# The steps of a chunked scan in another order around a split-precision MLP, and the halves of its output regrouped

## The chip, the cores and the metric

One core of a Trainium2 chip runs the whole program. The metric is the device time of one execution in microseconds. The profile is of one execution on the chip.

## The reference

A chunked state-space scan (Mamba2 SSD) is followed by an MLP with SiLU. Per batch and head, for each chunk of 32 positions:

```
cum = cumsum(log(clip(a)))             # x (4,8,768,32), a (4,8,768), B and C (4,8,768,16)
M   = (C B^T) * exp(cum_i - cum_j) * causal
y   = M x + (C state) * exp(cum)
state = exp(sum la) * state + sum_j B_j x_j * exp(cum_last - cum_j)
```

y is laid out as 3072 tokens of 256 values, and out = silu(y w_in) w_out, with w_in 256 x 2048 and w_out 2048 x 256, all fp32.

## The kernel before

**Units and pairs.** The scan works on twelve units of 256 positions, three to a batch, each in four chunks of 64. The MLP works on six pairs of two units, 512 tokens each. Every engine's instructions are in the order in which the program writes them (the schedule is manual), so an instruction that waits holds all that stand behind it on its engine. Each DMA queue is in order too; nearly all loads and all stores are on the sync engine's queue.

**The steps of a unit**, by the letters of the program's strings: L loads it. T transposes B and C (VectorE; for units 1 and 2 TensorE, in a PSUM tile tp) and ScalarE makes ce from ct. P makes the decay prefix pfx (VectorE). 0, 1, 2 make the decay matrix E: 0 clips a, 1 and 2 are two scans of VectorE. B makes BT from E's last column, C makes cw from ct (both GpSimd as a rule). G and g are the two halves of C B^T on TensorE, here called G(0) and G(1), into the one two-bank PSUM tile gy. M and m, here M(0) and M(1), multiply that half into E in place (VectorE). D makes the chunks' state sums on TensorE, S the running states and, before the change, also sm, two activations. Y and y are the two halves of the output on TensorE, each followed by X, a copy to xf (ScalarE). h, l, d split xf into three fp32r parts: xh (ScalarE), xl (GpSimd), xd (VectorE). E, BT, ce, cw and sm have one buffer each, and so has gy.

**The first pair's MLP** is in plain fp32 matmuls: f_s1 (16 calls, into hp) and f_s2 (m0 to m7, into oa). The scan of units 2 and 3 and the preparation of the weights are written between them by hand: w_size and w_bits bring the weights (s, b), and w_h, w_l, w_d split them into WH, WL, WD (h, l, d with a number, or wh, wl, wd in rows). f_out stores the result by way of o and ot; then the loads of units 4 and 5 are issued.

**The other five pairs**, 1 to 5, run in steps of one 128-column tile of d_ff: sixteen steps to a pair, f = 0 to 15. A step holds twelve 128x512 matmuls: four in s1_h, two in s1_d for the next step, whose result ScalarE scales in place before s1_h may add to it, and six in s2 of three steps earlier (LAG). Between them stand g and gh (ScalarE), gl (GpSimd) and gd (VectorE). At its end step f takes stage f of PLAN for the first unit of the next pair and stage f - 6 for its second unit:

```
    PLAN = ("T", "P0", "12GBC", "Mg", "mD", "S", "Y", "y", "hld")
...
            for i, base in enumerate((0, 6)):
                if 0 <= f - base < len(PLAN):
                    u = 2 * P + 2 + i
                    stage(u, PLAN[f - base])
```

So in step 8 the first unit's h, l, d are written ahead of the second unit's stage 2. f_out of a pair comes in step 2 of the next pair, after that step's s2; it holds two od on ScalarE and o, ot, o, ot on VectorE, and the next pair's s2 accumulates in the banks that od and o read.

Of the kernel before, what the change touches and what calls it, by code (L numbers as in the profile page):

```python
# [12 lines left out]
AF = mybir.ActivationFunctionType  # L13
# [18 lines left out]
def kernel(  # L32
# [22 lines left out]
    nc = tc.nc  # L55

    batch, H, S, D = x.shape
    N = B.shape[-1]
    Q = 64
    UT = 256  # L60
    UPB = S // UT
    NU = batch * UPB
    d_model, d_ff = moe_w_in.shape
    NF = d_ff // 128
# [88 lines left out]
    NW = 16  # L153
# [4 lines left out]
    def two(t):  # L158
        return t.rearrange("p (k f) -> p k f", k=2)
# [36 lines left out]
    def w_h(n):  # L196
        WH[n] = block("wh", F32R)
        nc.scalar.activation(WH[n], w32[n], AF.Copy, scale=DOWN / 4096.0)

    def w_l(n):  # L200
        WL[n] = block("wl", F32R)
        nc.vector.scalar_tensor_tensor(out=WL[n], in0=WH[n].bitcast(FP32), scalar=-4096.0, in1=w32.pop(n),
                                       op0=ALU.mult, op1=ALU.add)

    def w_d(n, engine=nc.gpsimd):
        WD[n] = block("wd", F32R)
        engine.tensor_tensor(out=WD[n], in0=WH[n].bitcast(FP32), in1=WL[n].bitcast(FP32), op=ALU.subtract)
# [207 lines left out]
    def f_S(u, t0=0, t1=4):  # L415
        first, last = u % UPB == 0, u % UPB == UPB - 1
        if first and t0 == 0:
            ST[u] = sc2.tile([128, 4, 64], FP32, name="st")
        if not last and t1 == 4:
            ST[u + 1] = sc2.tile([128, 4, 64], FP32, name="st")  # L420
        for t in range(t0, min(t1, 3 if last else 4)):
            k, c = divmod(t, 2)
            o = ST[u][:, t + 1] if t < 3 else ST[u + 1][:, 0]
            if first and t == 0:
                nc.vector.tensor_copy(out=o, in_=BX[u][c][:, k])
            else:
                nc.vector.scalar_tensor_tensor(out=o, in0=ST[u][:, t], scalar=PFX[u][:, t, Q:],
                                               in1=BX[u][c][:, k], op0=ALU.mult, op1=ALU.add)

    def f_SM(u):  # L430
        t0 = 1 if u % UPB == 0 else 0
        SM[u] = sc.tile([128, 4, 64], FP32, name="sm")
        for e in range(2):
            nc.scalar.activation(SM[u][:, t0:, 32 * e:32 * e + 32], ST[u][:, t0:, 32 * e:32 * e + 32],
                                 AF.Copy, scale=par[:, e:e + 1])

    def f_Y(u, w):
        sp, cw, m, xc = SM[u], CW[u], E[u], xt[u]
        y = GY[u] = bank2()
        opened = set()  # L440
        for t in ((1, 2, 3) if w == 0 else (2, 1, 3)) if u % UPB == 0 else range(4):
            k, c = divmod(t, 2)
            for q in range(2):
                g = 2 * w + q
                nc.tensor.matmul(out=y[64 * q:64 * q + 64, c, 64 * k:64 * k + 64],  # L445
                                 lhsT=sp[32 * g:32 * g + 32, t], rhs=cw[32 * g:32 * g + 32, Q * t:Q * t + Q],
                                 start=(c, q) not in opened, stop=False,
                                 tile_position=(32 * g, 64 * q), skip_group_check=True)
                opened.add((c, q))
        for k in range(2):  # L450
            for c in range(2):
                for q in range(4):
                    h = 4 * w + q
                    nc.tensor.matmul(out=y[32 * q:32 * q + 32, c, 64 * k:64 * k + 64],
                                     lhsT=xc[64 * c:64 * c + 64, k, h], rhs=m[64 * c:64 * c + 64, k, h],
                                     start=False, stop=True, tile_position=(64 * c, 32 * q), skip_group_check=True)

    def f_X(u, w):

        if w == 0:  # L460
            XF[u] = block("xf")
        y = GY.pop(u)
        nc.scalar.activation(two(XF[u])[:, w].rearrange("p (k c t) -> p c k t", k=2, c=2),
                             y[:, :, 0:128].rearrange("p c (k t) -> p c k t", k=2), AF.Copy)


    XH, XL, XD = {}, {}, {}
# [46 lines left out]
    G, GH, GL, GD, HP = {}, {}, {}, {}, {}  # L514

    def s1_d(s):
        P, f = 1 + s // NF, s % NF
        HP[s] = half("hp")
        for kc in range(KC):
            nc.tensor.matmul(out=HP[s], lhsT=two(WD[f // 2])[:, kc, 128 * (f % 2):128 * (f % 2) + 128], rhs=XD[P][:, kc],  # L520
                             start=(kc == 0), stop=False, skip_group_check=True)
        nc.scalar.activation(HP[s], HP[s], AF.Copy, scale=-1.0 / UP)  # L522

    def s1_h(s):
        P, f = 1 + s // NF, s % NF
        for kc in range(KC):
            for i, (w, x_) in enumerate(((WH, XH), (WL, XL))):
                nc.tensor.matmul(out=HP[s], lhsT=two(w[f // 2])[:, kc, 128 * (f % 2):128 * (f % 2) + 128],  # L528
                                 rhs=x_[P][:, kc], start=False, stop=(kc == KC - 1 and i == 1), skip_group_check=True)
        if f == NF - 1:  # L530
            for X in (XH, XL, XD):
                X.pop(P)
# [109 lines left out]
    def stage(u, what):  # L642
        for c in what:
            if c == "L":
                load_unit(u)
            elif c == "T":
                if 0 < u < UPB:
                    f_TP(u)
                else:
                    f_T(u, 0)  # L650
                    f_T(u, 1)
                f_T2(u, 0)
                f_T2(u, 1)
            elif c == "P":
                f_P(u)
            elif c == "0":
                f_E0(u, 0, 1)
            elif c in "12":
                f_E1(u, int(c) - 1, 2)
            elif c == "B":  # L660
                f_B(u)
            elif c == "C":
                f_C(u)
            elif c in "Gg":
                f_G(u, "Gg".index(c))
            elif c in "Mm":
                f_M(u, "Mm".index(c))
            elif c == "D":
                f_D0(u)
            elif c == "S":  # L670
                f_S(u)
                f_SM(u)
            elif c in "Yy":
                f_Y(u, "Yy".index(c))
                f_X(u, "Yy".index(c))
            elif c == "h":
                f_xh(u)
            elif c == "l":
                f_xl(u)
            elif c == "d":  # L680
                f_xd(u)

    def todo(text):

        for step in text.split():
            if ":" in step:
# [3 lines left out]
            n = int(step[1:].split(".")[0])  # L690
            {"b": w_bits, "s": w_size, "h": w_h, "l": w_l, "d": w_d, "m": f_s2, "o": partial(f_out, 0)}[step[0]](n)

    steps = ((1, 0, ""), (0, 3, "b5 s6"), (1, 1, "b6 s7"), (1, 2, "b7 s8"), (1, 3, "b8"), (0, 4, ""),
             (1, 4, "2:T"), (0, 5, "2:P012 2:B s9"), (1, 5, "2:CG b9 s10 2:M"), (0, 6, "2:g"), (1, 6, "b10 s11 2:m"),
             (0, 7, "2:D b11 2:S s12"), (1, 7, "2:Yy b12 s13"))
    for u, j, text in steps:
        f_s1(u, j)
        todo(text)
    stage(3, "L")
    for text in ("m0 2:h h0 2:l l0 2:d b13 s14", "m1 d0 b14 s15", "m2 h1 b15 3:T", "m3 l1 d1 3:P012", "m4 3:BC 3:G",  # L700
                 "m5 3:Mg 3:m h8 3:D l8 d8", "m6 3:S 3:Y", "m7 3:y 3:h 3:l 3:d h2 l2 d2 h9 l9 d9 o0 o1"):
        todo(text)
    stage(4, "L")
    stage(5, "L")
# [1 line left out]

    NP = NU // 2
    LAG = 3
    PLAN = ("T", "P0", "12GBC", "Mg", "mD", "S", "Y", "y", "hld")
    WAITING = []  # L710

    def step(s):

        last = NF * (NP - 1)
        if s < last:
            if s == 0:
                s1_d(0)
            s1_h(s)
            if s + 1 < last and (s + 1) % NF:
                s1_d(s + 1)  # L720
            s1_g(s)
            s1_gl(s)
        if s >= LAG:
            s2(s - LAG)
        if s - 1 >= 0 and s - 1 < last:
            s1_gd(s - 1)
        if s >= LAG and (s - LAG) % NF == NF - 1:
            P = 1 + (s - LAG) // NF
            f_out(P, 0)
            f_out(P, 1)  # L730
        if s >= last:
            return
        P, f = 1 + s // NF, s % NF
        if P + 1 < NP:
# [3 lines that stand above are left out]
                    stage(u, PLAN[f - base])  # L738
                    if PLAN[f - base] == "y" and u + 2 < NU:
                        load_unit(u + 2)  # L740
        if P == 1 and f % 2 == 0:
            for n in (3 + f // 2, 10 + f // 2):
                if n < (8 if n == 3 + f // 2 else NW):
                    w_h(n)
                    w_l(n)
                    w_d(n)
        if s + 1 < last and (s + 1) % NF == 0:
            s1_d(s + 1)

# [33 lines left out]
```

## Time and profile before

| | before |
|---|---|
| time, median of two runs | 461.23 us (460.69 to 461.77) |
| time of the profiled execution | 462.7 us |
| its span | 460.7 us |
| TensorE busy | 378.4 us (82%) |
| VectorE, ScalarE, GpSimd busy | 221.4 (48%), 213.1 (46%), 183.5 us (40%) |
| mean granted clock of TensorE | 0.904 of full speed |

The span lies inside the execution, which takes 2.0 us more. A matmul's row ends some time after the next one may start, so distances are read from start to start. PE is TensorE's matmuls, DVE VectorE, ACT ScalarE, POOL GpSimd and SP the sync engine's queue.

### The profile page before, as it was taken

To read this page: it belongs to the slowest core of one execution; us is meant where nothing else is said; L and a number is where in the kernel's file an instruction comes from. 1 tells how busy PE (TensorE), PEld (TensorE's weight loads), DVE (VectorE), ACT (ScalarE), POOL (GpSimd) and SP (SyncE) were. 2 spreads that over 40 slices of the span, in tenths; PEclk is the share of its full clock that TensorE was granted. 3 is DMA by queue.
4 is the path that set the end of the run, shared out by engine and by line. 5 is a ranking of instruction groups with operands and counts; after the bars stand their busy time and mean duration, and the time that the engine had idled before them with its cause. 6 is when DMAs were issued, how large, how long until landed. Compare 5 with 4: busy or idle time off the path is not lost. (4 is left out here: it accounts for less than half of the span.)

```text
span 460.7 us, 7904 instructions
## 1 busy us (share of the span) xinstructions
PE 378.4 (82%) x3145; PEld 284.1 (62%) x3146; DVE 221.4 (48%) x343; ACT 213.1 (46%) x403; POOL 183.5 (40%) x160
## 2 busy tenths in 40 slices
PE   7898989952499397969699769969787969799993
PEld 3577778731376275747477547657565747577882
DVE  7689659224858734354421463342364442324222
ACT  2567461043358074626336434616452625365660
POOL 3344344233667544323434242433333343334440
PEclk9999999977789798879979888979798989889998
DMA  8879630026650400044140035140011000002002
GB/s 183 185 198 278 171 55 1 1 35 127 125 104 27 82 9 0 2 87 74 35 81 1 0 65 96 36 81 3 0 19 28 1 1 1 1 0 47 0 1 46
DMA packets 112620, 26.35 MB, mean 57 GB/s; under 512 B 102216, under 2 KB 108360, under 8 KB 112584
## 3 DMA queue, kind: packets, MB, share of 16 engines
q1 hardware_dynamic: 110504, 25.73, 26.7%
q8 instruction: 24, 0.39, 0.4%
q10 hardware_dynamic: 2080, 0.13, 0.3%
q14 instruction: 12, 0.10, 0.1%
HBM read 22.70 MB, written 3.15 MB: 56 GB/s over the span
## 5 line engine op out<-in xcount | busy, mean ns | idle before, releaser
L542 POOL TENSOR_TENSOR gl<-g,gh 128x512 fp32r<-128x512 f32 x80 | 104.2, 1303 | 165.7 <-ACT gh L538 147.4
L546 DVE SCALAR_TENSOR_TENSOR gd<-gl,gh 128x512 fp32r<-128x512 f32 x80 | 61.5, 774 | 142.7 <-POOL gl L542 139.1
L522 ACT ACTIVATE hp<-hp 128x512 f32<-128x512 f32 x80 | 46.5, 582 | 160.2 <-PE hp L520 160.2
L528 PE MATMUL hp<-xh,wh 128*128 128x512 f32 x160 | 75.8, 474 | 12.2 <-ACT hp L522 12.2
L528 PE MATMUL hp<-xl,wl 128*128 128x512 f32 x160 | 70.1, 438 | 0.0
L520 PE MATMUL hp<-xd,wd 128*128 128x512 f32 x160 | 57.7, 446 | 13.5 <-DVE xd L483 13.5
L560 PE MATMUL oa<-gh,wh 128*128 128x512 f32 x160 | 65.8, 411 | 0.4 <-DVE o L570 0.4
L561 PE MATMUL oa<-gl,wl 128*128 128x512 f32 x160 | 65.0, 406 | 0.0
L557 PE MATMUL oa<-gd,wd 128*128 128x512 f32 x160 | 54.6, 424 | 0.1
L407 PE MATMUL gy<-ce,bh 32*64 32x128 f32 x384 | 19.6, 323 | 41.3 <-DVE E L413 41.3
L538 ACT ACTIVATE gh<-g 128x512 fp32r<-128x512 f32 x80 | 50.5, 631 | 3.7
L528 PEld LDWEIGHTS hp<-xh,wh 128*128 128x128 f32 x160 | 33.9, 212 | 28.0 <-ACT hp L522 16.5
L520 PEld LDWEIGHTS hp<-xd,wd 128*128 128x128 f32 x160 | 34.0, 215 | 23.6 <-DVE xd L483 15.4
L536 ACT ACTIVATE g<-hp 128x512 f32<-128x512 f32 x80 | 47.5, 593 | 1.0 <-PE hp L528 0.6
L407 PEld LDWEIGHTS gy<-ce,bh 32*64 32x64 f32 x384 | 12.7, 155 | 49.9 <-DVE E L413 42.8
L557 PEld LDWEIGHTS oa<-gd,wd 128*128 128x128 f32 x160 | 33.4, 209 | 9.0 <-DVE o L570 0.5
L560 PEld LDWEIGHTS oa<-gh,wh 128*128 128x128 f32 x160 | 32.3, 202 | 9.4 <-DVE o L570 1.8
L528 PEld LDWEIGHTS hp<-xl,wl 128*128 128x128 f32 x160 | 34.4, 215 | 5.9
L561 PEld LDWEIGHTS oa<-gl,wl 128*128 128x128 f32 x160 | 31.8, 199 | 7.6
L191 POOL TENSOR_TENSOR w<-wu,wv 128x512 uint32<-128x512 uint32 (+1 forms) x20 | 21.7, 1093 | 31.9 <-DVE wv L186 30.9
L493 PE MATMUL hp<-xf,w 128*128 128x256 f32 x128 | 30.1, 386 | 2.6 <-DVE cw L375 1.8
L483 DVE SCALAR_TENSOR_TENSOR xd<-xl,xh 128x512 fp32r<-128x512 f32 x10 | 11.1, 1106 | 41.7 <-POOL xl L479 41.7
(82 smaller groups left out, 452.9 us busy)
## 6 DMA issues: line engine op xcount, KB each, us to landing
ab<-in_a_dram SPq DMA_DIRECT2D x40, 128.0 KB
raw<-in_moe_w_in_dram SPq DMA_DIRECT2D x8, 512.0 KB
raw<-in_moe_w_out_dram SPq DMA_DIRECT2D x8, 512.0 KB
xt<-in_x_dram SPq DMA_DIRECT2D x24, 128.0 KB
out_dram<-ot SPq DMA_DIRECT2D x48, 64.0 KB
bn<-in_B_dram SPq DMA_DIRECT2D x22, 64.0 KB
tbc<-in_C_dram SPq DMA_DIRECT2D x40, 32.0 KB
pa<-in_a_dram SPq DMA_DIRECT2D x10, 128.0 KB
```

The lines of the kernel that those rows point to most:

```text
L407: nc.tensor.matmul(out=GY[u][64 * c:64 * c + 64, q, 128 * k:128 * k + 128], lhsT=bh[32 * g:32 * g + 32, ts], rhs=ce[32 * g:32 * g + 32, :, ...
L493: nc.tensor.matmul(out=hp[:, i], lhsT=two(w32[j])[:, kc, 128 * i:128 * i + 128], rhs=two(XF[u])[:, kc], start=(kc == 0), stop=(kc == KC - 1))
L520: nc.tensor.matmul(out=HP[s], lhsT=two(WD[f // 2])[:, kc, 128 * (f % 2):128 * (f % 2) + 128], rhs=XD[P][:, kc], start=(kc == 0), stop=Fals ...
L522: nc.scalar.activation(HP[s], HP[s], AF.Copy, scale=-1.0 / UP)
L528: nc.tensor.matmul(out=HP[s], lhsT=two(w[f // 2])[:, kc, 128 * (f % 2):128 * (f % 2) + 128], rhs=x_[P][:, kc], start=False, stop=(kc == KC ...
L536: nc.scalar.activation(G[s], HP.pop(s), AF.Silu, scale=UP)
L538: nc.scalar.activation(GH[s], G[s], AF.Copy, scale=DOWN)
L542: nc.gpsimd.tensor_tensor(out=GL[s], in0=G.pop(s), in1=GH[s].bitcast(FP32), op=ALU.subtract)
L546: nc.vector.scalar_tensor_tensor(out=GD[s], in0=GL[s].bitcast(FP32), scalar=-4096.0, in1=GH[s].bitcast(FP32), op0=ALU.mult, op1=ALU.add)
L557: nc.tensor.matmul(out=OA[P][1][m], lhsT=two(WD[n])[:, r, ms], rhs=gd, start=(f == 0), stop=(f == NF - 1))
L560: nc.tensor.matmul(out=OA[P][0][m], lhsT=two(WH[n])[:, r, ms], rhs=gh, start=(f == 0), stop=False)
L561: nc.tensor.matmul(out=OA[P][0][m], lhsT=two(WL[n])[:, r, ms], rhs=gl, start=False, stop=(f == NF - 1))
```

## The change

The program writes the scan's stages in another order, in the five pairs' PLAN and in the hand-written part before it. T and P go into one stage, E, its scans and B into the next, then G(0), C and M(0), then G(1) and M(1), then D and S; sm is a stage of its own (s). Unit 3's loads and steps are written earlier in the first pair's part. Weight parts 3 to 7 are made in the first pair's second product and not in pair 1; parts 10 to 15 are made in two steps each. In the step in which a pair's last s2 comes, that s2 is written ahead of s1_h. And f_Y(u, e) makes, where it made four heads over both chunk parities, both head halves w, each at chunk parity w ^ e, one PSUM bank to a head half; so the first sixteen matmuls take four row and column tiles of the array by turns instead of two. f_X copies a bank at a time, in two activations instead of one.

```diff
-    def f_Y(u, w):
+    def f_Y(u, e):
...
-        for t in ((1, 2, 3) if w == 0 else (2, 1, 3)) if u % UPB == 0 else range(4):
-            k, c = divmod(t, 2)
-            for q in range(2):
-                g = 2 * w + q
-                nc.tensor.matmul(out=y[64 * q:64 * q + 64, c, 64 * k:64 * k + 64],
-                                 lhsT=sp[32 * g:32 * g + 32, t], rhs=cw[32 * g:32 * g + 32, Q * t:Q * t + Q],
-                                 start=(c, q) not in opened, stop=False,
-                                 tile_position=(32 * g, 64 * q), skip_group_check=True)
-                opened.add((c, q))
         for k in range(2):
-            for c in range(2):
+            for w in range(2):
+                t = 2 * k + (w ^ e)
+                if t == 0 and u % UPB == 0:
+                    continue
+                for q in range(2):
+                    g = 2 * w + q
+                    nc.tensor.matmul(out=y[64 * q:64 * q + 64, w, 64 * k:64 * k + 64],
+                                     lhsT=sp[32 * g:32 * g + 32, t], rhs=cw[32 * g:32 * g + 32, Q * t:Q * t + Q],
+                                     start=(w, q) not in opened, stop=False,
+                                     tile_position=(32 * g, 64 * q), skip_group_check=True)
+                    opened.add((w, q))
+        for k in range(2):
+            for w in range(2):
+                c = w ^ e
                 for q in range(4):
                     h = 4 * w + q
-                    nc.tensor.matmul(out=y[32 * q:32 * q + 32, c, 64 * k:64 * k + 64],
+                    nc.tensor.matmul(out=y[32 * q:32 * q + 32, w, 64 * k:64 * k + 64],
                                      lhsT=xc[64 * c:64 * c + 64, k, h], rhs=m[64 * c:64 * c + 64, k, h],
                                      start=False, stop=True, tile_position=(64 * c, 32 * q), skip_group_check=True)
 
-    def f_X(u, w):
+    def f_X(u, e):
...
-        nc.scalar.activation(two(XF[u])[:, w].rearrange("p (k c t) -> p c k t", k=2, c=2),
-                             y[:, :, 0:128].rearrange("p c (k t) -> p c k t", k=2), AF.Copy)
+        o = two(XF[u]).rearrange("p w (k c t) -> p w k c t", k=2, c=2)
+        for w in range(2):
+            nc.scalar.activation(o[:, w, :, w ^ e], y[:, w, 0:128].rearrange("p (k t) -> p k t", k=2), AF.Copy)
...
             elif c == "S":
                 f_S(u)
+            elif c == "s":
                 f_SM(u)
...
-    steps = ((1, 0, ""), (0, 3, "b5 s6"), (1, 1, "b6 s7"), (1, 2, "b7 s8"), (1, 3, "b8"), (0, 4, ""),
-             (1, 4, "2:T"), (0, 5, "2:P012 2:B s9"), (1, 5, "2:CG b9 s10 2:M"), (0, 6, "2:g"), (1, 6, "b10 s11 2:m"),
-             (0, 7, "2:D b11 2:S s12"), (1, 7, "2:Yy b12 s13"))
+    steps = ((1, 0, ""), (0, 3, "b5 s6"), (1, 1, "b6 s7"), (1, 2, "b7 s8"), (1, 3, "b8"), (0, 4, "2:T"),
+             (1, 4, "2:P0"), (0, 5, "2:12B s9 3:L"), (1, 5, "2:GCM b9 s10"), (0, 6, "2:gm"), (1, 6, "2:DS b10 s11"),
+             (0, 7, "2:s 2:Y b11 s12"), (1, 7, "2:y b12 s13 3:T"))
...
-    stage(3, "L")
-    for text in ("m0 2:h h0 2:l l0 2:d b13 s14", "m1 d0 b14 s15", "m2 h1 b15 3:T", "m3 l1 d1 3:P012", "m4 3:BC 3:G",
-                 "m5 3:Mg 3:m h8 3:D l8 d8", "m6 3:S 3:Y", "m7 3:y 3:h 3:l 3:d h2 l2 d2 h9 l9 d9 o0 o1"):
+    for text in ("m0 2:h h0 3:P0 2:l b13 s14", "m1 3:12B 2:d h1 l0 d0 b14 s15", "m2 3:GCM l1 d1 h2", "m3 3:gm b15 l2 d2 h3",
+                 "m4 3:DS l3 d3 h4", "m5 3:s 3:Y l4 d4 h5", "m6 3:y 3:h 3:l l5 d5 h6 3:d h8", "m7 l8 l6 d8 d6 h7 h9 l7 l9 d7 d9 o0 o1"):
...
-    PLAN = ("T", "P0", "12GBC", "Mg", "mD", "S", "Y", "y", "hld")
+    PLAN = ("TP", "012B", "GCM", "gm", "DS", "s", "Y", "y", "hld")
...
+            if s >= LAG and (s - LAG) % NF == NF - 1:
+                s2(s - LAG)
             s1_h(s)
...
-        if s >= LAG:
+        if s >= LAG and (s >= last or (s - LAG) % NF != NF - 1):
             s2(s - LAG)
...
-        if P == 1 and f % 2 == 0:
-            for n in (3 + f // 2, 10 + f // 2):
-                if n < (8 if n == 3 + f // 2 else NW):
-                    w_h(n)
-                    w_l(n)
-                    w_d(n)
+        n = 10 + f // 2
+        if P == 1 and n < NW:
+            if f % 2 == 0:
+                w_h(n)
+            else:
+                w_l(n)
+                w_d(n)
```

## Rows read from the trace of the kernel before

**Rows 1.** Second product, pair 1, pair 3 by windows: busy us (instructions), clock:

```profile
61.38:97.48 36.10, 31.92 (x290) 26.62 (x281) 19.72 (x29) 10.80 (x22) 12.30 (x11) 0.98 0.01 1
99.37:183.25 83.88, 57.99 (x487) 42.08 (x487) 48.40 (x59) 38.52 (x73) 47.16 (x35) 0.85 0.38 70
256.96:328.89 71.93, 60.40 (x497) 45.03 (x497) 29.76 (x50) 33.85 (x64) 26.62 (x22) 0.88 0.24 45
```

**Rows 2.** List of waits: engine, line, tile, awaited; us in total, times, longest:

```profile
PE gy L407 <- DVE E L413: 41.3, 10, 7.9
...
PE hp L493 <- DVE cw L375: 1.8, 1, 1.8
```

**Rows 3.** TensorE, pair 3, steps 9 to 11: start us, us, instruction, [idle before]:

```profile
298.26 0.39 PE L561 MATMUL oa<-gl,wl 128*128 128x512 f32 x1
302.92 1.15 PE L407 MATMUL gy<-ce,bh 32*64 32x128 f32 x16 [4.27 <-DVE E L413]
...
309.09 0.50 PE L528 MATMUL hp<-xh,wh 128*128 128x512 f32 x1
...
311.98 0.39 PE L528 MATMUL hp<-xh,wh 128*128 128x512 f32 x1
```

**Rows 4.** Timeline of VectorE and GpSimd in the same stretch:

```profile
296.78 1.30 POOL L479 TENSOR_TENSOR xl<-xf,xh 128x512 fp32r<-128x512 f32 x1
...
298.12 0.69 DVE L483 SCALAR_TENSOR_TENSOR xd<-xl,xh 128x512 fp32r<-128x512 f32 x1 [4.54 <-POOL xl L479]
...
298.73 2.33 DVE L314 TENSOR_TENSOR_SCAN E<-ab,diag 128x512 f32<-128x512 f32 x2
...
301.14 1.00 POOL L347 TENSOR_TENSOR BT<-bn,E 128x256 f32<-128x256 f32 x1 [3.05 <-DVE E L314]
```

**Rows 5.** Timeline of VectorE and GpSimd at the end of pair 3:

```profile
325.60 1.28 POOL L542 TENSOR_TENSOR gl<-g,gh 128x512 fp32r<-128x512 f32 x1
325.69 1.73 DVE L483 SCALAR_TENSOR_TENSOR xd<-xl,xh 128x512 fp32r<-128x512 f32 x1 [4.38 <-POOL xl L479]
```

**Rows 6.** Timeline of pair 3, steps 2 to 4, three engines:

```profile
267.31 1.06 ACT L569 ACTIVATE od<-oa 128x512 f32<-128x512 f32 x2
...
267.48 0.50 PE L528 MATMUL hp<-xh,wh 128*128 128x512 f32 x1
...
267.92 0.69 DVE L570 SCALAR_TENSOR_TENSOR o<-oa,od 128x512 f32<-128x512 f32 x1 [0.76 <-ACT od L569]
...
268.65 0.71 DVE L572 STREAM_TRANSPOSE ot<-o 128x512 f32<-128x512 f32 x1
...
274.76 1.15 PE L407 MATMUL gy<-ce,bh 32*64 32x128 f32 x16 [4.04 <-DVE E L413]
```

**Rows 7.** Timeline from the first pair's end to step 2 of pair 1:

```profile
97.48 1.22 PE L520 MATMUL hp<-xd,wd 128*128 128x512 f32 x2 [3.30 <-DVE xd L483]
...
98.55 1.30 DVE L572 STREAM_TRANSPOSE ot<-o 128x512 f32<-128x512 f32 x2
...
99.28 4.40 SPq L574 DMA_DIRECT2D out_dram<-ot  x8
...
109.67 0.64 DVE L352 STREAM_TRANSPOSE ct<-tbc 128x256 f32<-128x256 f32 x1 [0.96 <-DMA tbc<-in_C_dram]
...
112.82 0.80 PE L528 MATMUL hp<-xh,wh 128*128 128x512 f32 x1 [8.18 <-ACT hp L522]
```

**Rows 8.** Timeline of TensorE, step 3 of pair 1:

```profile
125.65 1.15 PE L407 MATMUL gy<-ce,bh 32*64 32x128 f32 x16 [5.87 <-DVE E L413]
```

**Rows 9.** Timeline of TensorE in pair 3, one Y and what follows:

```profile
287.05 0.68 PE L445 MATMUL gy<-cw,sm 32*64 32x64 f32 x16
287.66 0.45 PE L454 MATMUL gy<-E,xt 64*32 64x64 f32 x32
288.04 0.50 PE L528 MATMUL hp<-xh,wh 128*128 128x512 f32 x1
```

**Rows 10.** Timeline of TensorE in the opening:

```profile
12.19 0.68 PE L407 MATMUL gy<-ce,bh 32*64 32x128 f32 x16 [2.07 <-DVE E L413]
```

More of the change, by code (lines that the diff above doesn't have):

```diff
@@ L452, in f_Y @@
+        for k in range(2):
+            for w in range(2):
+                c = w ^ e
                 for q in range(4):
                     h = 4 * w + q
-                    nc.tensor.matmul(out=y[32 * q:32 * q + 32, c, 64 * k:64 * k + 64],
+                    nc.tensor.matmul(out=y[32 * q:32 * q + 32, w, 64 * k:64 * k + 64],
                                      lhsT=xc[64 * c:64 * c + 64, k, h], rhs=m[64 * c:64 * c + 64, k, h],
                                      start=False, stop=True, tile_position=(64 * c, 32 * q), skip_group_check=True)
-    def f_X(u, w):
-        if w == 0:
+    def f_X(u, e):
+        if e == 0:
```

## The prediction, made before the change was run

> **What bounds the kernel now.** I read the busy table first: TensorE is busy 82% of the span, the others under half. So TensorE sets the time, and what counts is its idle time and its clock. The windows by stage come next. Pair 1 takes 83.9 us and pair 3 71.9 us, each with a mean granted clock of 0.85 to 0.88 [rows 1]. A step that carries no scan work takes 2.89 us at full clock (two starts of the xh matmul, 309.09 and 311.98) [rows 3], so sixteen take 46 us. The scan's own matmuls explain few of the other 26 us of pair 3. The list of waits names the rest: TensorE stands 41.3 us, in ten waits, ahead of G(1), because VectorE's M(0) is late [rows 2]. 2.6 us of that lie in the opening (one of 2.07 us stands in [rows 10]); the other 38.7 are 5.87 [rows 8] and 7.90 [rows 2] in pair 1 and 4.04 [rows 6] and 4.27 [rows 3] in each of pairs 2 to 4. A second cost follows each: from G(1) at 302.92 to the second step after it TensorE takes 6.17 us [rows 3], where G(1) at 0.68 [rows 10], one step of 2.89 and a D of 0.38 (32 small matmuls, as in [rows 9]) make 3.95. So a long wait costs 2.2 us more at the low one of TensorE's two clocks.
>
> Why M(0) is late, the timelines of VectorE and GpSimd show: xl ends 298.08, then xd, then two E scans of 2.33 us together, then BT of 1.00 on GpSimd, which must read E before M(0) overwrites it [rows 4]. All of that stands between TensorE's arrival (298.26 plus one matmul) and its G(1).
>
> **The change, part by part.**
>
> *The scan's steps in a pair.* E, its two scans and BT move one step earlier, and M(0) goes into the step of G(0), ahead of G(1) by a whole step. What is late then?
>
> Second unit of a pair (steps 8 and 9). In step 8 VectorE still has xd of the first unit ahead of M(0), since the first unit's last stage is written before the second's. E has one buffer, so the scans can't start before the first unit's second Y is done, at the start of step 8; they and BT (1.00) then push gl and xl by up to 0.9 us. M(0) follows xl (298.08) by xd, 0.69 alone [rows 4] or 1.73 beside a GpSimd operation [rows 5], and by its own 0.78 (BT's end to G(1), 302.14 to 302.92). That is 299.6 to 301.5; TensorE is there at 298.65. The wait of 4.27 becomes 0.9 to 2.9 us; I take 2.0, the middle, since both pushes are likely in part.
>
> First unit (steps 2 and 3). The scans are out of the way, but f_out isn't: od, o, ot, o, ot of the pair that ends stand ahead of M(0). And the last s2 now goes ahead of s1_h in step 2. ScalarE's queue has the next scale, g and gh of that step before od, and they wait for s1_h, which comes 1.4 us later (six matmuls, half a step). So od moves from 267.31 [rows 6] to 268.7; o follows by 0.6, the four VectorE operations take 2.7 (two of 0.69 and two of 0.71), M(0) ends at 272.8. TensorE has done step 3 at 270.3 (267.48 plus 2.8). Behind o wait the next pair's s2 matmuls, which need its accumulators, and behind M(0) G(1): together 2.5 us, for 4.04 now. Ends: 1.1 if f_out keeps its old time, 4.0 if nothing is gained.
>
> Pairs 2 to 4: 8.31 becomes 4.5, so -3.8 each, **-11.4**. Pair 1 has no f_out in its step 2: the wait of 5.87 goes (-5.9). For its second unit a weight part (about 1.3 on GpSimd, as a gl) still stands ahead of gl: 7.9 becomes 3.1 (-4.8). Together **-10.7**.
>
> *The clock.* A wait of 2.07 us in the opening left G(1) at 0.68 us, full speed, where it took 1.15 after 4.27 [rows 3, 10]. I take it that six of the remaining waits (2.0, and 2.5 in pieces) leave the clock up and that the 3.1 doesn't: seven times 2.2, **-15.4**. The other end is one time, -2.2.
>
> *Weight parts.* Five triples (n = 3 to 7) leave pair 1 for the first pair's second product, where in 36.1 us VectorE is busy 19.7, ScalarE 10.8 and GpSimd 12.3 [rows 1]. A triple adds about 0.7, 0.5 and 1.3 to them (as an xd, an od and a gl): this cover holds. If VectorE were full, each part would put 0.7 us onto the way to ot.
>
> *Unit 3 earlier.* Its last Y ends before the eighth part of the second product, not after it. X, xh, xl, xd run beside matmuls, and the 3.30 us wait of the first xd matmul [rows 7] goes. But step 2 of pair 1 waits (8.18 us) for a scale that is queued behind ce, which needs unit 4's C; that load is issued after the eight output issues (4.40 us), which wait for ot at 98.55 [rows 7]. Only ot's time counts. TensorE has finished the second product and Y at 94.18 now (97.48 less 3.30). It should get there about 2.5 us sooner, since unit 2's steps wait less (1.8 us for C, the last reader of tp's bank [rows 2], is the largest wait; an estimate between 0 and 3.4): 91.7. Four weight parts of 0.7 to 0.9 us stand ahead of ot on VectorE: ot at 94.9 for 98.55, so C's transpose 3.65 earlier than 109.67, and one wh (0.6) fewer is ahead of the scale: step 2 starts **4.2** earlier. Ends: 0 (VectorE full) and -6. Unit 3's loads pass nothing on the sync queue: all weight loads are issued before them in both orders.
>
> *Halves of y.* Y's first 16 matmuls take 0.61 us over two tiles of the array by turns, the next 32 take 0.38 over eight [rows 9]. Over four tiles I take 0.36, so 0.25 saved in each of 16 Ys of the loop, **-4.0**; ends 0, and 0.42 each (12 ns a matmul). X becomes two activations; ScalarE is busy under half of the time, and bank and XF are next needed a step later: nothing. In the opening, where y waits for X, it may cost 0.2 each, as much as Y gives.
>
> *s2 ahead of s1_h in pair 5.* No G(0) covers the scale there (0.6 us with its signals, as long as one od [rows 6]), and o comes 1.4 later: **+1.3**, from 0 to 2.
>
> Sum: -11.4 - 10.7 - 15.4 - 4.2 - 4.0 + 1.3 = -44.4. The profiled execution took 462.7 us, 0.3% over the median of 461.2; I apply the sum to the median: **417 us**.
>
> **A rule against it.** GpSimd's gl and VectorE's two-input operations disturb each other: xd takes 0.69 us with GpSimd idle and 1.73 beside a gl [rows 4, 5]. The E scans ran beside an idle GpSimd so far; in the step before they stand beside a gl. If each pair of scans gives up one gl (1.28 us [rows 5]) the eight units lose 10 us: 427. The Trainium skill states this (SBUF — State Buffer, section Who interferes with whom): a VectorE instruction with two SBUF inputs and a GpSimd instruction that reads SBUF exclude each other for a whole instruction. The xd rows agree; that a scan counts as such no row here shows.
>
> **Rivals.** (1) The clock still falls at the six remaining waits: +13.2, 430 us. For it: a wait of 4.04 did it each time, and 2.5 in pieces is busy for little of its stretch; against it, the 2.07. (2) The remaining waits vanish, since f_out and xd fit into the slack: 18.8 less, 398 us. Against it: xd and M(0) are in one queue behind xl. (3) The lock above, 427 us. (4) Slower: many short waits keep TensorE at its low clock through the scan's steps 3 to 13 of all four pairs, 44 steps at 2.2 us: 514 us. It decides from 24 low steps on (417 + 24 x 2.2 = 470). Against it: after each wait the clock was back within two steps [rows 3]. That Y gains nothing is inside the range (421).
>
> **How the numbers follow.** Forecast 0.52; clock 0.22; lock 0.12; waits gone 0.12; slower 0.02. Range 400 to 434: rival 1 plus Y's 4 at the top, just above rival 2 at the bottom. A change under 2% is what this measurement can't tell from none; that would be above 452, which takes the clock rival, no Y, no earlier start and full waits at once: faster 0.95, same 0.03, slower 0.02.
>
> **What would show it.** G(1) rows with waits of 2 us instead of 4 and a length of 0.68; step 2 of pair 1 starting near 108.6 (112.82 now); Y's 16 matmuls in about 0.36 us; od 1.4 us later after step 2's start, o ahead of the next pair's gh matmul; the wait for xd at the ends of pairs unchanged. Wrong: G(1) still waiting 4 us for M(0), or low-clock steps after it.

## The result, and the profile after

The changed kernel takes 431.37 us (median of two runs, 429.31 to 433.42) where the kernel before takes 461.23. The ratio is 0.935, with a 95% interval of 0.916 to 0.955. The forecast was 417 us with a range of 400 to 434. The profiled execution took 429.31 us (span 427.6); the one before took 462.7 (span 460.7). Ratios leave out executions that lie over 1.5% above the fastest of their kernel (one of e2, two of e3 and one of c1 below; the profiled ones of e2 and e3 are such), so there they differ from the quotient of the two medians.

The stretches of [rows 1], after: the first pair's second product, then pairs 1 to 4. The columns are busy us and instructions of TensorE, its weight load, VectorE, ScalarE and GpSimd, then the granted clock, the DMA share and GB/s.

```profile
64.19:98.40 34.21, 32.75 (x293) 26.50 (x283) 25.11 (x36) 14.21 (x31) 19.24 (x15) 1.00 0.00 1
98.40:176.30 77.90, 55.20 (x486) 40.20 (x486) 41.34 (x56) 36.25 (x72) 42.09 (x32) 0.85 0.40 75
176.30:238.90 62.60, 55.98 (x505) 40.94 (x505) 33.76 (x52) 34.02 (x68) 27.54 (x22) 0.96 0.27 51
238.90:305.30 66.40, 59.84 (x497) 43.69 (x497) 32.56 (x50) 34.02 (x68) 27.20 (x22) 0.91 0.26 49
305.30:367.70 62.40, 55.84 (x505) 40.87 (x505) 33.11 (x49) 34.08 (x68) 26.99 (x22) 0.97 0.06 9
```

Pair 3 went from 71.9 us at a clock of 0.88 to 66.4 at 0.91, and pairs 2 and 4 take 62.5 at 0.96 and 0.97. Pair 1 went only from 83.9 to 77.9, and its clock is still 0.85. The second product starts at 64.19, 2.8 us later than before.

The list of waits of the changed kernel (us in total, times, longest):

```profile
PE gy L407 <- DVE E L413: 17.0, 10, 4.0
...
PE hp L527 <- DVE xd L490: 11.0, 5, 2.5
...
PE hp L500 <- DVE cw L375: 3.7, 1, 3.7
```

TensorE's 41.3 us ahead of G(1) [rows 2] are 17.0 now. Its wait for xd at the ends of pairs, which the prediction left as it was, comes close behind with 11.0. The wait in the opening for the bank of tp went the wrong way, from 1.8 to 3.7.

**The second unit of a pair.** Step 8 of pair 3, timeline of TensorE, VectorE and GpSimd (start, duration, instruction, idle before it); compare [rows 3, 4]:

```profile
269.82 1.28 POOL L549 TENSOR_TENSOR gl<-g,gh 128x512 fp32r<-128x512 f32 x1 [2.21 <-ACT gh L545]
...
270.24 3.05 DVE L314 TENSOR_TENSOR_SCAN E<-ab,diag 128x512 f32<-128x512 f32 x2 [0.73 <-PE gy L460]
...
273.38 1.01 POOL L347 TENSOR_TENSOR BT<-bn,E 128x256 f32<-128x256 f32 x1 [2.27 <-DVE E L314]
...
274.35 1.29 POOL L549 TENSOR_TENSOR gl<-g,gh 128x512 fp32r<-128x512 f32 x1
...
275.60 1.30 POOL L486 TENSOR_TENSOR xl<-xf,xh 128x512 fp32r<-128x512 f32 x1
...
276.93 1.16 DVE L490 SCALAR_TENSOR_TENSOR xd<-xl,xh 128x512 fp32r<-128x512 f32 x1 [3.06 <-POOL xl L486]
...
278.01 0.68 DVE L413 TENSOR_TENSOR E<-gy,E 128x512 f32<-128x512 f32 x1
...
278.75 1.15 PE L407 MATMUL gy<-ce,bh 32*64 32x128 f32 x16 [2.07 <-DVE E L413]
279.82 0.79 PE L535 MATMUL hp<-xh,wh 128*128 128x512 f32 x1
```

Read it backwards from G(1): M(0) had its input from G(0) since 273.7, BT was done with E at 274.4, and from then on M(0) waited for its place on VectorE, behind xd; xd waited for xl, xl stood on GpSimd behind gl, and gl behind BT. That is the chain that the prediction wrote down, and the wait is 2.07 where it said 2.0. The same wait stands in pairs 2 and 4. What differs is what follows it: here G(1) takes 1.15 and the next xh matmul 0.79, the low clock, and the next two steps are long (6.19 and 5.91 us), as behind the waits of 4 us before the change. In pair 2 the clock stayed up (5.73 and 3.36):

```profile
215.16 0.68 PE L407 MATMUL gy<-ce,bh 32*64 32x128 f32 x16 [2.07 <-DVE E L413]
215.78 0.50 PE L535 MATMUL hp<-xh,wh 128*128 128x512 f32 x1
```

**The first unit of a pair.** Pair 3, steps 2 and 3, same columns, TensorE, ScalarE and VectorE; compare [rows 6]:

```profile
250.73 0.50 PE L535 MATMUL hp<-xh,wh 128*128 128x512 f32 x1
...
251.81 1.07 ACT L576 ACTIVATE od<-oa 128x512 f32<-128x512 f32 x2
...
252.42 0.69 DVE L577 SCALAR_TENSOR_TENSOR o<-oa,od 128x512 f32<-128x512 f32 x1 [1.39 <-PE hp L527]
252.44 0.49 PE L564 MATMUL oa<-gd,wd 128*128 128x512 f32 x1
...
253.17 0.50 PE L564 MATMUL oa<-gd,wd 128*128 128x512 f32 x1 [0.23 <-DVE o L577]
...
254.49 0.50 PE L567 MATMUL oa<-gh,wh 128*128 128x512 f32 x1 [0.36 <-DVE o L577]
...
255.11 0.65 DVE L413 TENSOR_TENSOR E<-gy,E 128x512 f32<-128x512 f32 x1
...
255.81 0.68 PE L407 MATMUL gy<-ce,bh 32*64 32x128 f32 x16 [0.59 <-DVE E L413]
```

The wait of 4.04 has become three small ones, two for o and one for M(0), and the clock stays up. od comes 1.08 after the first xh matmul of step 3, where it came 0.17 before it (267.31 against 267.48) [rows 6]: 1.25 later, by the s2 that now stands ahead of s1_h.

**The start of pair 1.** From the end of the second product to the first G(1) of pair 1, all engines and the sync queue; compare [rows 7, 8]:

```profile
95.18 1.75 DVE L490 SCALAR_TENSOR_TENSOR xd<-xl,xh 128x512 fp32r<-128x512 f32 x1 [5.17 <-POOL xl L486]
...
96.86 4.67 DVE L202 SCALAR_TENSOR_TENSOR wl<-wh,w 128x512 fp32r<-128x512 f32 x4
96.99 0.73 PE L527 MATMUL hp<-xd,wd 128*128 128x512 f32 x2 [0.79 <-DVE xd L490]
...
98.02 5.88 POOL L207 TENSOR_TENSOR wd<-wh,wl 128x512 fp32r<-128x512 f32 x4 [1.63 <-DVE wl L202]
...
101.45 1.29 DVE L579 STREAM_TRANSPOSE ot<-o 128x512 f32<-128x512 f32 x2
...
102.18 4.38 SPq L581 DMA_DIRECT2D out_dram<-ot  x8
...
112.50 0.64 DVE L352 STREAM_TRANSPOSE ct<-tbc 128x256 f32<-128x256 f32 x1 [1.08 <-DMA tbc<-in_C_dram]
...
115.14 0.79 PE L535 MATMUL hp<-xh,wh 128*128 128x512 f32 x1 [12.75 <-ACT hp L529]
...
118.27 0.69 DVE L330 TENSOR_SCALAR ab<-ab 128x1024 f32<-128x1024 f32 x1 [3.69 <-DMA ab<-in_a_dram]
...
123.85 0.68 PE L407 MATMUL gy<-ce,bh 32*64 32x128 f32 x16 [2.07 <-DVE E L413]
```

The first xd matmul comes half a microsecond sooner (96.99 against 97.48) and its wait is 0.79 for 3.30, but ot comes 2.9 us later (101.45 against 98.55): four wl stand ahead of it on VectorE and take 4.67 us beside the wd on GpSimd. The first two of them took 0.68 each, with GpSimd idle or just starting; the third, beside wd, took 1.79, and the third and fourth together 3.47. What hangs on ot follows at the distance of before, but for the one wh fewer ahead of the scale (0.5 us). The eight output issues take 4.38 us, C lands, ct, then step 2 at 115.14, 2.3 us later than before. The same late loads hold up VectorE at unit 4's ab for 3.69 us; M(0) stands behind it on VectorE, and G(1) waits 2.07 for M(0), where the prediction had no wait.

**Y's first sixteen matmuls**, pair 3, TensorE; compare [rows 9]:

```profile
265.52 0.46 PE L450 MATMUL gy<-cw,sm 32*64 32x64 f32 x16
265.91 0.45 PE L460 MATMUL gy<-E,xt 64*32 64x64 f32 x32
266.30 0.50 PE L535 MATMUL hp<-xh,wh 128*128 128x512 f32 x1
```

They take 0.39 us from start to start, 0.22 less than before.

### The profile page after: what moved, and what is told of

The parts are those of the page before. It is cut to its first block, busy times and chain, and to the rows that moved or that the text cites. A ratio compares the mean times of both kernels' runs of the same rounds, so it can differ in the third digit from the quotient of the medians.

```text
span 427.6 us, 7952 instructions
## 1 busy us (share of the span) xinstructions
PE 362.9 (85%) x3146; PEld 268.8 (63%) x3146; DVE 228.6 (53%) x343; ACT 214.5 (50%) x427; POOL 185.8 (43%) x160
## 4 chain that ended last, share of the span: by engine, by line
PE 62%; DVE 12%; issue 10%; POOL 6%; ACT 5%; SPq 2%; DMA 1%; DVEq 0%; POOLq 0%; ACTq 0%
PE hp L535 17%; PE hp L527 8%; PE oa L564 7%; PE oa L567 7%; PE oa L568 7%; PE oa L513 4%; PE hp L500 4%; PE gy L407 3%; POOL xl L486 2%; DVE xd L490 2%; POOL gl L549 2%; DVE E L413 2%; DVE o L577 2%; PE gy L450 2%; PE gy L460 2%
## 5 line engine op out<-in xcount | busy, mean ns | idle before, releaser
L549 POOL TENSOR_TENSOR gl<-g,gh 128x512 fp32r<-128x512 f32 x80 | 108.0, 1350 | 156.9 <-ACT gh L545 127.2
L535 PE MATMUL hp<-xh,wh 128*128 128x512 f32 x160 | 71.7, 448 | 17.6 <-ACT hp L529 17.4
L535 PE MATMUL hp<-xl,wl 128*128 128x512 f32 x160 | 66.6, 416 | 0.0
L527 PE MATMUL hp<-xd,wd 128*128 128x512 f32 x160 | 54.4, 423 | 11.0 <-DVE xd L490 11.0
L535 PEld LDWEIGHTS hp<-xh,wh 128*128 128x128 f32 x160 | 31.6, 197 | 31.9 <-ACT hp L529 22.2
L527 PEld LDWEIGHTS hp<-xd,wd 128*128 128x128 f32 x160 | 31.9, 202 | 20.7 <-DVE xd L490 13.1
L314 DVE TENSOR_TENSOR_SCAN E<-ab,diag 128x512 f32<-128x512 f32 x24 | 34.5, 1475 | 7.1 <-PE gy L460 6.8
L535 PEld LDWEIGHTS hp<-xl,wl 128*128 128x128 f32 x160 | 32.1, 200 | 5.3
L490 DVE SCALAR_TENSOR_TENSOR xd<-xl,xh 128x512 fp32r<-128x512 f32 x10 | 14.0, 1400 | 35.1 <-POOL xl L486 35.1
L407 PE MATMUL gy<-ce,bh 32*64 32x128 f32 x384 | 17.4, 294 | 17.0 <-DVE E L413 17.0
```

Of the source, the lines that this page charges most:

```text
L314: nc.vector.tensor_tensor_scan(out=E[u].rearrange("p k h t -> p (k h t)")[:, Q * g0:Q * (g0 + n)], data0=t.rearrange("p g t -> p (g t)"), ...
L549: nc.gpsimd.tensor_tensor(out=GL[s], in0=G.pop(s), in1=GH[s].bitcast(FP32), op=ALU.subtract)
```

## The experiments

Twelve kernels ran, in three groups, each group on one chip, with four executions of each kernel (ten of e9) and the kernel before on the same chip (461.3, 462.9 and 462.1 us, medians). Ratios are against that. Step lengths are from the start of one step's first xh matmul to the next step's. The first group takes the prediction's parts one at a time.

**e2_s2_back**: the last s2 of a pair stands behind s1_h again.

```diff
-            if s >= LAG and (s - LAG) % NF == NF - 1:
-                s2(s - LAG)
             s1_h(s)
...
-        if s >= LAG and (s >= last or (s - LAG) % NF != NF - 1):
+        if s >= LAG:
             s2(s - LAG)
```

> The changed kernel with a pair's last s2 behind s1_h again, as before the change. Theory: this part costs time, since od waits in ScalarE's queue for an s1_h that comes 1.4 us later; the three waits of steps 2 to 4 (0.23 + 0.36 + 0.59) and the wait for the scale in pair 5 go, about 1.2 us in each of pairs 2 to 5: 4 to 5 us faster than the changed kernel, od about 1.4 us earlier after the start of step 2's first matmul. Rival: f_out isn't what stands ahead of M(0) but the E scans do; then the waits only move and the time stays within 1.5 us.

425.71 us (421.39 to 427.91), ratio 0.920 [0.914, 0.925]. Pair 3, steps 2 and 3:

```profile
252.39 0.68 DVE L577 SCALAR_TENSOR_TENSOR o<-oa,od 128x512 f32<-128x512 f32 x1
...
253.33 0.63 PE L564 MATMUL oa<-gd,wd 128*128 128x512 f32 x2
...
255.76 0.68 PE L407 MATMUL gy<-ce,bh 32*64 32x128 f32 x16 [0.58 <-DVE E L413]
```

od starts 0.17 us ahead of step 3's first xh matmul again, as before the change, and the two gd matmuls of the next pair's s2 run without a wait; the wait for M(0) stays. Steps 1 to 3 of pair 3 take 2.78, 3.48 and 4.55 us, where the changed kernel has 4.34, 2.23 and 5.70. In pair 5 steps 1 to 3 take 2.78, 2.78 and 3.78 for 4.15, 2.23 and 4.34: 1.4 us. So the new place of s2 costs 1.0 to 1.5 us in each of pairs 2 to 5, and the change would be faster without it.

**e3_m_first**: in each step the second unit's stage is written ahead of the first unit's, so M(0) ahead of xh, xl and xd.

```diff
-            for i, base in enumerate((0, 6)):
+            for i, base in ((1, 6), (0, 0)):
```

> The changed kernel with the second unit's stage written ahead of the first unit's in every step, so that in step 8 M(0) stands ahead of xd on VectorE. Theory: G(1) of the second unit waits 2.07 us because M(0) is queued behind xl and xd; now the wait goes in pairs 2 to 4 and falls from 4.04 to about 2 in pair 1, and no low clock follows it: 8 us faster (6.2 + 2.0, and up to 4 more where the clock fell). Rival: M(0) is late because of BT, which waits for E's scans, which wait for the first unit's y; then G(1) still waits about 1.5 to 2 us and the time stays within 2 us.

419.91 us (415.61 to 426.89), ratio 0.903 [0.900, 0.905]. Step 8 of pair 3:

```profile
271.86 0.69 DVE L413 TENSOR_TENSOR E<-gy,E 128x512 f32<-128x512 f32 x1 [0.54 <-POOL BT L347]
...
274.04 0.68 PE L407 MATMUL gy<-ce,bh 32*64 32x128 f32 x16
...
275.01 1.77 DVE L490 SCALAR_TENSOR_TENSOR xd<-xl,xh 128x512 fp32r<-128x512 f32 x1 [2.46 <-POOL xl L486]
...
278.08 0.46 PE L392 MATMUL gy<-xt,BT 64*32 64x64 f32 x32 [0.38 <-issue]
```

M(0) is done 1.5 us ahead of G(1), which waits for nothing; step 9 takes 3.58 for 6.19 (5.73 in pairs 2 and 4), and 0.38 appears at D. So it was the place behind xd, not the scans or BT, that set the wait of 2.07. In pair 1 the wait of 4.04 goes too, but a wait of 3.00 at D takes most of its place.

**e4_old_y**: f_Y and f_X as before the change (the diff of the change, reversed in these two functions).

> The changed kernel with f_Y and f_X as before the change. Theory: the regrouping takes about 0.22 us off every Y in the loop (sixteen), so this is 3 to 4 us slower than the changed kernel, with Y's first sixteen matmuls back at 0.61 us for 0.39. Rival: the second activation of X gives it back (opening and first pair, where y waits for X), and the time stays within 1.5 us.

435.50 us (432.89 to 437.40), ratio 0.945 [0.942, 0.948]; the steps that hold a Y are 0.22 longer again (3.87 and 3.97 for 3.65 and 3.75), but only 0.12 in the two units that begin a batch (3.75 and 3.86 for 3.63 and 3.74), where Y starts with twelve matmuls and not sixteen. Twelve times 0.22 and four times 0.12 are 3.1 us, and the median is 4.1 above the changed kernel's.

**e1_loads_first**: the loads of units 4 and 5 are written ahead of the first pair's f_out.

```diff
-    ... "m7 l8 l6 d8 d6 h7 h9 l7 l9 d7 d9 o0 o1"):
+    ... "m7 l8 l6 d8 d6 h7 h9 l7 l9 d7 d9"):
...
+    todo("o0 o1")
```

> The changed kernel with one order altered: the loads of units 4 and 5 are written ahead of the first pair's f_out, so that they stand ahead of its eight output issues on the sync queue. Theory: step 2 of pair 1 waits 12.75 us because unit 4's C lands late behind those outputs, and those wait on VectorE behind four weight parts; then the wait nearly goes, step 2 starts near 103 instead of 115.1, and the time falls by 9 to 13 us against the changed kernel (to about 418 to 422). Rival: the wait is for VectorE or ScalarE work (weight parts, ce) and not for the loads; then T of unit 4 still starts after 108 and the time stays within 3 us of 431.

419.81 us (418.92 to 421.35), ratio 0.910 [0.908, 0.913].

```profile
101.48 1.29 DVE L579 STREAM_TRANSPOSE ot<-o 128x512 f32<-128x512 f32 x2
...
103.15 0.61 DVE L352 STREAM_TRANSPOSE ct<-tbc 128x256 f32<-128x256 f32 x1
...
105.76 0.79 PE L535 MATMUL hp<-xh,wh 128*128 128x512 f32 x1 [3.32 <-ACT hp L529]
```

ot is where it was (101.48) but ct follows at 103.15, 9.4 us sooner: C is no longer issued behind the eight output issues. Step 2 starts at 105.76 for 115.14. This shows that ot and the output issues set the start of pair 1, and that 3.3 of the 12.75 us hang on something else: ct is still behind ot on VectorE.

The second group asks how far executions differ, what the plan alone gives, and what stands ahead of ot.

**a2_again**: the changed kernel a second time, on another chip.

> The changed kernel once more, as the yardstick on the same chip: about 431 us, single executions 429 to 434, since waits of 2.07 us and of 2.54 us lower TensorE's clock in some executions and not in others.

432.81 us (428.82 to 434.60), ratio 0.933 [0.926, 0.940]. The waits at the second unit's G(1) are the same (2.08, 2.06, 2.06), but the clock fell after none of them: in pair 3 steps 9 and 10 took 5.72 and 3.36, where they took 6.19 and 5.91.

In the opening it was the other way round. From the end of the wait for C (3.74 us in the first profile, 3.73 here) to the second product, columns as above, in the first profile:

```profile
48.41:64.19 15.78, 14.51 (x201) 11.05 (x201) 8.69 (x16) 9.10 (x18) 4.33 (x4) 1.00 0.50 101
```

and here:

```profile
48.55:67.22 18.67, 17.40 (x200) 13.11 (x201) 8.69 (x16) 9.07 (x18) 4.32 (x4) 0.84 0.36 64
```

The same work takes 2.9 us more at a mean clock of 0.84. Of the eleven profiled executions that have this wait of 3.7 us, the clock fell behind it in seven (to a mean of 0.84 to 0.90); in the three with a wait of 1.8 or 1.9 there (the kernel before, e5_plan_only and e7_T_back) it stayed at 1.00.

**e5_plan_only**: the kernel before with the new PLAN and nothing else of the change; sm stays with S in the hand-written part.

```diff
-    PLAN = ("T", "P0", "12GBC", "Mg", "mD", "S", "Y", "y", "hld")
+    PLAN = ("TP", "012B", "GCM", "gm", "DS", "s", "Y", "y", "hld")
```

> The kernel before with nothing changed but the PLAN of the five pairs (stages one step earlier, sm on its own); first pair, weight parts, Y and s2 as before the change. Theory: nearly all of the gain comes from here; pairs 2 to 4 as in the changed kernel less what the s2 order costs and plus what the old Y costs, and pair 1 with its eleven weight parts keeps waits: 428 to 436 us. Rival: the weight parts made early carry much of the gain, since they keep VectorE and GpSimd in pair 1 too late for M(0); then 440 us or more, with waits at G(1) of 4 us and over in pair 1.

436.17 us (431.78 to 437.75), ratio 0.940 [0.933, 0.947]. Pairs 2 to 4 take 64.3, 61.8 and 64.5 us. Pair 1 takes 80.6: with five more weight parts in it, two wd on GpSimd hold up gl, gl holds up gd and gd the transpose of unit 5's C on VectorE, and step 8 starts with a wait of 4.05 us for a scale that is queued behind ce.

**e6_store_first**: f_out ahead of the last weight parts in the eighth part of the second product.

```diff
-    "m7 l8 l6 d8 d6 h7 h9 l7 l9 d7 d9 o0 o1"
+    "m7 o0 o1 l8 l6 d8 d6 h7 h9 l7 l9 d7 d9"
```

> The changed kernel with the first pair's f_out written ahead of the last part's weight parts (l8 l6 l7 l9 on VectorE), nothing else. Theory: ot starts at 101.5 because of the four weight parts (96.9 to 101.5); here near 97, unit 4's C 4 us sooner, step 2 of pair 1 near 111 instead of 115.1: 4 to 5 us faster than the changed kernel. Rival: what holds unit 4's loads is not ot's time; then within 1.5 us.

426.99 us (426.37 to 427.87), ratio 0.921 [0.915, 0.927].

```profile
114.83 0.79 PE L535 MATMUL hp<-xh,wh 128*128 128x512 f32 x1 [6.42 <-ACT hp L529]
```

The second product began at 68.31 here (64.19 in the changed kernel's profile, 67.22 in a2_again), so distances from it count: step 2 starts 46.5 us after it, for 50.9 in both executions of the changed kernel. So 4.4 us of the start of pair 1 are the weight parts ahead of ot.

**c1_no_f0**: the edits of e1, e2 and e3 together.

> The changed kernel with three edits together: loads of units 4 and 5 ahead of the outputs, a pair's last s2 behind s1_h again, the second unit's stage ahead of the first's. If the three act in different places their gains add up: 431 less 11, 5 and 10 is about 405 us. If they share a wait, 408 to 415 us.

404.81 us (402.32 to 412.06), ratio 0.872 [0.866, 0.878]. Against a2_again's 432.81 that is 28.0; the three alone, each against its own chip's runs of before, are 0.023, 0.014 and 0.031 below a2_again's ratio, some 31 us. They add up, nearly.

The third group.

**e7_T_back**: unit 2's T is written one call of the first product later, where it was before the change.

```diff
-    ... (0, 4, "2:T"),
-    (1, 4, "2:P0"), ...
+    ... (0, 4, ""),
+    (1, 4, "2:TP0"), ...
```

> The changed kernel with unit 2's T one f_s1 later, where it stood before the change. Theory: the 3.74 us wait of an f_s1 for C (the last reader of tp's bank) is T made early: C comes no sooner, so TensorE only runs against the held bank earlier; the wait goes back to about 1.8 us, the second product starts 1.5 to 2 us sooner, and since pair 1's step 2 hangs on the outputs behind it the time falls by about 2 us, which is at the limit of what the runs tell. Rival: the wait is set by C itself and the rest of the first pair absorbs it: the second product starts at the same time, no change.

426.33 us (425.89 to 429.52), ratio 0.925 [0.919, 0.930].

```profile
48.18 1.99 PE L500 MATMUL hp<-xf,w 128*128 128x256 f32 x8 [1.86 <-DVE cw L375]
...
62.26 0.92 PE L513 MATMUL oa<-gT,w 128*128 128x256 f32 x3
```

In the changed kernel this wait is 3.74 and ends at 48.41, and the second product starts at 64.19. T's matmuls take the bank of tp 1.6 us sooner there, and the reader, ct and then cw on VectorE, doesn't come sooner. Moving T gives back 1.9 us, at the second product's start and at step 2 (113.19 for 115.14) alike. Against a2_again, where the clock fell behind the longer wait, the way from the wait's end to the second product is 4.6 us shorter (14.08 for 18.67). The medians differ by 5.0 and 6.5; how many of the executions without a profile had the low clock there isn't known.

**e9_first_only**: the change's first part and weight parts with the old PLAN, the old Y and the old place of s2.

> The other side of the kernel with the PLAN alone: the first pair's part and the weight parts as in the change, but PLAN, Y and s2 as before it (sm right behind S). Theory: the first pair's part gives nothing by itself, since ot and with it unit 4's loads come later; what pair 1 saves by five weight triples fewer (waits at G(1) of 5.87 and 7.90 us shrink by 1 to 3 each) is about what the start loses: 455 to 463 us. Rival: the weight parts are a main cause of pair 1's 84 us; then 450 us or less.

460.14 us (457.00 to 463.00), ratio 0.996 [0.992, 0.999]. Alone, the rewritten first part gives about nothing: pair 1 takes 81.5 us for 83.9, with a wait of 12.64 for its step 2. Pairs 2 to 4 are as before (71.7, 71.6, 72.0).

**e8_split_early**: the second unit's h, l, d are written in step 13, behind its second Y, and not in step 14.

```diff
-                    stage(u, PLAN[f - base])
+                    stage(u, PLAN[f - base] if not i or f < 13 else ("yhld", "")[f - 13])
```

> The changed kernel with h, l, d of a pair's second unit written in step 13, right behind its second Y, and not in step 14. Theory: the 2.54 us wait for xd at the end of pairs 1 to 4 is queue order, since xh stands behind the g and gh of step 14, xl behind their gl; here xd is done 3 us sooner, the wait goes and the low clock after it too: 2.54 and 1 to 2 us in each of four pair ends, 12 to 17 us faster than the changed kernel. Rival: the split's three operations in a row set it; then gl and gd of steps 13 and 14 come later instead and the time stays within 3 us.

408.69 us (407.91 to 409.33), ratio 0.885 [0.881, 0.888]. The end of pair 2:

```profile
226.54 1.31 POOL L486 TENSOR_TENSOR xl<-xf,xh 128x512 fp32r<-128x512 f32 x1 [0.27 <-ACT xh L483]
...
227.88 0.69 DVE L490 SCALAR_TENSOR_TENSOR xd<-xl,xh 128x512 fp32r<-128x512 f32 x1 [4.62 <-POOL xl L486]
...
230.36 0.63 PE L527 MATMUL hp<-xd,wd 128*128 128x512 f32 x2
```

xd is done 1.8 us before TensorE wants it; in the changed kernel TensorE waits 2.54 us for it. The last step takes 3.62 for 6.42 and the next pair's first 2.88 for 4.4 to 5.3. So a wait of 2.54, and the low clock behind it, cost 4.2 to 5.4 us in each of four pairs, more than the wait's own length.

**c2_split_early**: the edits of e1, e2, e3 and e8 together.

> All edits that helped, together: loads ahead of outputs, the last s2 behind s1_h, the second unit's stage first, and the split of the second unit in step 13. The three made 404.8 us; with the pair ends free of the wait for xd, 389 to 394 us. If the pair ends were held by something else, 402 to 405.

388.16 us (387.62 to 388.89), ratio 0.841 [0.837, 0.844]: faster than both kernels, by 74 and 43 us. Pairs 1 and 2:

```profile
102.40:162.00 59.60, 52.51 (x487) 38.50 (x487) 41.16 (x54) 36.26 (x72) 41.89 (x32) 0.94 0.29 54
162.00:217.70 55.70, 53.69 (x504) 39.83 (x504) 32.90 (x50) 34.22 (x68) 27.32 (x23) 1.00 0.31 58
```

Pairs 2 to 4 run at a clock of 1.00 with TensorE busy 96% of the time, and the four executions lie within 1.3 us.

## Why the prediction was right, and which terms were off

The forecast of faster held, by the mechanism that it names: TensorE sets the time, M(0) on VectorE held it up, and a new order takes out the long waits and the low clock that follows them. e5 shows that PLAN alone brings 27 us (462.9 to 436.2; the whole change 30.1 on the same chip), and e9 that the first part alone brings about 2. The profiled execution, stretch by stretch, against the prediction's terms:

| stretch | predicted | measured |
|---|---|---|
| up to step 2 of pair 1 | -4.2 | +2.3 |
| the rest of pair 1 (waits -10.7, clock -2.2, Y -1.0) | -13.9 | -9.2 |
| pairs 2 to 4 (waits -11.4, clock -13.2, Y -3.0) | -27.6 | -26.3 |
| pair 5 | +1.3 | +0.1 |
| sum | -44.4 | -33.1 |

The measured column goes by the spans (460.7 to 427.6). The medians differ by 29.9, since 429.31 is the lower of two runs that lie 4.1 apart. That the time fell inside the range is in part luck: its upper part was there for a clock that stays low at the six waits, and what filled it is the start of pair 1 (6.5 us) and the rest of pair 1 (4.7).

*The step that failed: the start of pair 1.* The prediction had ot at 94.9; it came at 101.45. It put TensorE's end of the second product at 91.7, from a start 2.5 us sooner; TensorE came to its xd wait at 96.2 (96.99 less 0.79), since the start was 2.8 us later. 1.9 of that is T's bank (e7): the prediction had named the wait for C as the one that would shrink, with T's move on record in the diff, and not asked who needs that bank next. 1.1 lies ahead of the first product, which began at 19.66 for 18.55, and there profiled executions of one order differ too: in e5, whose code up to there is that of the kernel before, it began at 23.53. The second error is of size. Four weight parts were put at 0.7 to 0.9 us each on VectorE; they took 4.67, and the two that ran beside wd about 1.75 each. The prediction had this price in its own rows, 0.69 for an xd alone and 1.73 beside a gl, and used it for the scans and not for wl. e6 and e1 show both that this chain set the start of pair 1 and what it is worth: 4.4 us for the parts ahead of ot, 9.4 for C's place behind the output issues.

*Pair 1's waits.* 2.07 and 4.04 stand where 0 and 3.1 were predicted, 3.0 us more. The first stands behind ab's 3.69: that f_out is missing in step 2 of pair 1 was right, but the late loads took its place. The low clock after it made step 4 4.93 long for 3.37 in pair 2, another 1.6. Together these are 4.6 of the 4.7 by which the row is off. Part of the 2.07 would be there without ab: in a2_again TensorE ran at its low clock for longer after the long wait for the scale, met no wait at G(1), and G(1) stood as far from step 2's start (8.77 us, for 8.71 here); in e1, with ab on time, 9.25. What a2_again saves against this execution is the second fall of the clock.

*Pairs 2 to 4.* Second unit: 2.0 predicted, 2.07 measured, by the chain BT, gl, xl, xd, M(0) (e3 shows that the place of M(0) decides). First unit: 2.5 predicted, 0.23 + 0.36 + 0.59 measured. The two small ones cost more than they show, some 0.5 each from start to start (252.44 to 253.17, where two such matmuls stand 0.23 apart), so it is about 1.6. od came 1.25 later for 1.4. *The clock* came back in five of the six places here, in all six in a2_again. Where it fell, in pair 3, the two steps took 3.0 us more. That is rival 1 in one place out of six, and it is one reason why executions of this kernel lie up to 6 us apart; the clock in the opening (a2_again) is another. Over the nine profiled executions that keep a wait of 1.8 to 2.1 us at the second unit's G(1), the clock fell behind it in 10 of 27 places, all three in e2. So rival 1 holds in part, and a2_again's none is no rule. The sum of the row is also nearer than its terms: by the rows above the waits gave some 13.9 for 11.4, the clock 10.2 for 13.2 and Y 2.2 for 3.0.

*Y* gave 0.22 each for 0.25, and 0.12 in the two units that begin a batch, 3.1 us for 4.0; e4 confirms it. *s2 ahead of s1_h* costs 1.4 in pair 5, as e2's steps show and as predicted (+1.3). The row shows only +0.1 because the stretch at low clock at pair 5's start was shorter this time (its first step took 4.33 for 5.29). But the prediction counted this cost in pair 5 alone as a loss. It costs as much in pairs 2 to 4, where it was hidden in the 2.5.

*The lock* (rival 3) exists, but is smaller than the 10 us set for it. The E scans took 3.05 beside a gl of 1.28, for 2.33 alone [rows 4]: 0.7 in the second units of pairs 2 to 4, inside the wait of 2.07. The Trainium skill (SBUF — State Buffer, section Who interferes with whom) says that a VectorE instruction with two SBUF inputs and a GpSimd instruction that reads SBUF exclude each other for a whole instruction. The rows agree that a scan belongs to these. The price is what gl still had to run: it began 0.42 ahead of the scans, 0.86 of it were left, and the first scan took 1.94 for 1.22. Where a whole gl fell into the scans, in the first units of pairs 2 and 4 and the second of pair 1, they took 3.39. That is some 5 us of VectorE's time in all; in the first units TensorE lost nothing by it, since its wait for M(0) is 0.59 in pair 3 too, where the scans took 2.34.

*What the prediction left alone.* It wrote that the wait for xd at the ends of pairs would be unchanged, and it was (2.54, four times). e8 shows that this was the largest thing left: 22 us by the ratios (0.885 for a2_again's 0.933), 18 of them in the steps around the four pair ends.

What stays open: what decides whether the clock falls after a wait of 2.07, or of 3.7 in the opening, and why the first product starts at different times.

## What to carry to other kernels

On an engine whose queue is in order, ask of a step that is late not only what it needs but what is written ahead of it: M(0) behind xd, C's load behind the stores, and xd written a step too late were each an edit of a line or two, and each alone gave, by the ratios, some 14, 11 and 22 us where the whole change had given 30. Price operations that run beside another engine's from a row in which they do so (a wl took 0.68 alone and 1.79 beside a wd), and when a producer is moved earlier, look for who needs its buffer next. A wait of TensorE costs its own length and then, often, some steps at the low clock, so the last waits of 2 to 3 us were worth as much as the longer ones here: with none above 0.7 left, pairs 2 to 4 ran at 1.00.

## What the runs showed of the hardware

The same wait of 2.07 us ahead of G(1) left TensorE at its high clock in pairs 2 and 4 (0.68 for G(1)) and at the low one in pair 3 (1.15); in a second run of the same kernel the clock fell in none of the three pairs, and in e2 in all three. A wait of about 4 us in pair 1 was followed by the low clock in both runs; a wait of 3.7 us in the opening was followed by it in the second (a mean of 0.84 to the second product) and not in the first (1.00).

Sixteen small matmuls over four tiles of the array by turns took 0.39 us, over two tiles 0.61.

A wl takes 0.68 us alone, a GpSimd operation of wd's kind (gl) 1.28; of four wl in a row the one that began beside a wd took 1.79, and four wd took 5.88. Two E scans took 3.05 beside the last 0.86 us of a gl, 3.39 with a whole gl beside them, and 2.34 in step 1 of pair 3, where the gl that started beside their end took 2.04 for 1.28.
